# Down phase of a two-layer mixture of experts: expert 0 in the first pass, scaled one product ahead of its cast

## The chip, the cores and the metric

One core of one Trainium2 chip runs the kernel. The metric is the device time of one execution in microseconds; of several executions the median counts.

## The reference, cut to what matters

The kernel computes attention, a first mixture of experts in which each token goes to one expert, and a second one in which every token goes through all eight. The change touches only the second product of the second mixture:

```python
def _moe2_ref(x, w_gate, w1, w2):
    N, D = x.shape                      # 2304, 512
    E = w_gate.shape[1]                 # 8; F = 1024
    P = np.exp(x @ w_gate - ...)        # then 8 rounds of row and column scaling
    out = np.zeros((N, D), dtype=np.float32)
    for e in range(E):
        h = np.maximum(x @ w1[e], 0.0)
        ye = h @ w2[e]
        out += P[:, e:e + 1] * ye
    return out
```

## The kernel before, in words

The second mixture runs in two phases, each written as a two-by-two block product of Strassen's kind with seven products (numbered b = 0 to 6) in place of eight. The **up phase** makes h of all experts, and writes it to the DRAM tensor `hd`, which holds for each expert e, each third u of a token half and each b one block of 128 x 1536 floats (768 KB). For experts 1 to 7 the blocks are already scaled by the token's weight P and already combined to the operand that product b needs. For expert 0 the weights P are not known yet in the up phase: its four plain parts are stored (h11 under 0, h12 under 2, h22 under 6, h21 under 4), and the **down phase** scales and combines them.

The down phase runs from about 1327 us to the end. `PASS` splits the experts into two groups of four; within a pass the b's run in the order `DORD` = 0, 3, 1, 2, 4, 6, 5, within a b the four experts, and within an expert the thirds u = 0, 1, 2. `STEPS` lists (pass, b, expert), `SEQ` the 168 products (step m, third u), numbered n from 0; pass 1 is n = 0 to 83, pass 2 is 84 to 167, and each b has twelve products (b 0 of pass 1: 0 to 11, b 3: 12 to 23, b 1: 24 to 35, b 2: 36 to 47, b 4: 48 to 59, b 6: 60 to 71, b 5: 72 to 83; pass 2 the same from 84, except that the last two experts alternate in its last b). The products of the last of four experts in a b are so 9 to 11, 21 to 23, 33 to 35, 45 to 47, ... In the kernel before, expert 0 is the last of the second pass (in its last b, the first).

One product is 24 matmuls (line 1405): operands are split into a high part, made by a cast, and a residual, high x high first, then residual of the weight x high, then weight x residual of h. What feeds a product:

- `h_make(n)` (line 1280): takes the stage slot with product n's block, and calls `both` (line 939): ACT casts the high part into one of four buffers `D["h"]` (line 937), VectorE subtracts for the residual (line 941). For expert 0 it first combines and scales on VectorE (line 944, through `op2`): the "source work" below. `SRC` says which stored parts each b needs: one for b 0, 4, 6, two for b 3, 1, 2, 5. Scaled results that a later b needs are written back to `hd` on POOL's DMA queue (line 1298), and the next weights p are loaded on SyncE's queue (`p_load`, line 1101) into one of two buffers.
- `h_load(n)` (line 1268): issues loads from `hd` on SyncE's queue into the four stage slots in turn, up to four loads beyond product n's first. `h_make(n)` ends with `h_load(n + 1)`. A load waits until the slot's last readers are done: cast, residual, and a write-back from it.
- `w_make(m)` (line 1252): for b 3, 1, 2 and 6 a weight difference or sum on VectorE (line 944), then `both` for the weight block, into one of two buffers `D["w"]`.
- `merge` (line 1371): after the last expert of a b, VectorE adds the accumulated bank to the output blocks, at most two additions per product.

The order on each engine is the order in which the program calls these (no scheduler reorders them): in the loop's step n the matmuls of product n, then merges, then `h_make(n + 3)`, then, where u = 1, `w_make(m + 1)`, then weight loads.

The lines of the loop that set it:

```python
            h_make(n + 3)
            j = m % 4
            if m < NM - 3:
                if u == 1:
                    w_make(m + 1)
```

Of the kernel before, what the change touches and what calls it, by code (L numbers as in the profile page):

```python
# [13 lines left out]
ALU = mybir.AluOpType  # L14
# [4 lines left out]
B, H, S, D = 4, 8, 576, 64  # L19
# [78 lines left out]
def _program(ctx, tc, qT, kT, vv, tau, wg, mod, mbias, cst, wA, wg2, wU, wD, out):  # L98
# [3 lines left out]
    V, A, G = nc.vector, nc.scalar, nc.gpsimd  # L102
# [5 lines left out]
    hd = dram.tile([E, NU, 7, P, 4, UN], F32, name="hd")  # L108
# [50 lines left out]
    def bc(ap, shape):  # L159
        return ap.to_broadcast(shape)  # L160
# [614 lines left out]
    def experts(es):  # L775
# [157 lines left out]
        def copy_on(eng, out, in_):  # L933
            if eng is G:
                G.tensor_scalar(out=out, in0=in_, scalar1=1.0, scalar2=1.0, op0=ALU.mult, op1=ALU.mult)
            else:
                A.copy(out=out, in_=in_)  # L937

        def both(hi_lo, src, cp, sub):
            copy_on(cp, hi_lo[0], src)  # L940
            sub.tensor_tensor(out=hi_lo[1], in0=src, in1=hi_lo[0].bitcast(F32), op=ALU.subtract)  # L941

        def op2(eng, out, x, y, op):
            eng.tensor_tensor(out=out, in0=x, in1=y, op=op)  # L944
# [154 lines left out]
        def load_p(dst, e, u):  # L1099
            for t in range(2):  # L1100
                nc.sync.dma_start(
                    out=dst[t], in_=pd[t].rearrange("(e u t) n -> e u (t n)", e=E, u=NU)[e, u].partition_broadcast(P))
# [88 lines left out]
        def gates():  # L1191
# [18 lines left out]

        xs, steps, later = chained(xs, make_x(1), make_x(2)), gates(), sink()
        D = {}
        PASS = ((1, 2, 3, 4), (5, 6, 7, 0))
        DORD = (0, 3, 1, 2, 4, 6, 5)
        STEPS = [(i, b, e) for i, es4 in enumerate(PASS) for b in DORD
                 for e in (es4 if (i, b) != (1, 5) else es4[3:] + es4[:3])]
        NM = len(STEPS)
        SEQ = [(m, u) for m in range(NM - 2) for u in range(NU)] + [(m, u) for u in range(NU) for m in (NM - 2, NM - 1)]
        NB = len(SEQ)
        SRC = {0: (0,), 3: (6, 2), 1: (3, 0), 2: (2, 0), 4: (4,), 6: (6,), 5: (4, 1)}  # L1220
        LOADS = [(n, b) for n, (m, u) in enumerate(SEQ)
                 for b in (SRC[STEPS[m][1]] if STEPS[m][2] == 0 else STEPS[m][1:2])]
        FIRST = {}
        for i, (n, _) in enumerate(LOADS):
            FIRST.setdefault(n, i)
        SCALED = [n for n, (m, u) in enumerate(SEQ) if STEPS[m][2] == 0 and STEPS[m][1] in (0, 3, 2, 4, 6)]
        NST = 4
        loaded = [0]

# [18 lines left out]
        def w_load(i, j, k):  # L1248
            nc.sync.dma_start(out=D["blk"][j, k],
                              in_=wD[PASS[i][j], :, 1024 * k:1024 * k + 1024].rearrange("p (k n) -> p k n", k=4))  # L1250

        def w_make(m):
            if m >= NM:
                return
            i, b, e = STEPS[m]
            j = PASS[i].index(e)
            w11, w12, w21, w22 = (D["blk"][j, k] if (j, k) in D["blk"] else None for k in range(4))
            if b == 3:
                op2(V, w21, w11, w21, ALU.subtract)
            elif b == 1:  # L1260
                op2(V, w21, w22, w21, ALU.subtract)
            elif b == 2:
                op2(V, w11, w21, w11, ALU.add)
            elif b == 6:
                op2(V, w12, w12, w21, ALU.subtract)
            both(D["w"][m % 2], {0: w11, 3: w21, 1: w21, 2: w11, 4: w12, 6: w12, 5: w22}[b], A, V)

        def h_load(n):
            top = FIRST.get(n, len(LOADS)) + NST
            while loaded[0] < min(top, len(LOADS)):  # L1270
                k, b = LOADS[loaded[0]]
                m, u = SEQ[k]
                nc.sync.dma_start(out=D["stage"][loaded[0] % NST], in_=hd[STEPS[m][2], u, b])
                loaded[0] += 1

        def p_load(i):
            if i < len(SCALED):
                load_p(pbs[i % 2], 0, SEQ[SCALED[i]][1])

        def h_make(n):  # L1280
            if n < NB:
                m, u = SEQ[n]
                _, b, e = STEPS[m]
                x = D["stage"][FIRST[n] % NST]
                if e == 0:
                    y = D["stage"][(FIRST[n] + 1) % NST]
                    if b == 3:
                        op2(V, x, x, y, ALU.subtract)
                    if n in SCALED:
                        i = SCALED.index(n)  # L1290
                        op2(V, x, x, bc(pbs[i % 2][0 if b in (0, 4) else 1].unsqueeze(1), [P, 4, UN]), ALU.mult)
                        p_load(i + 2)
                    if b == 1:
                        op2(V, x, x, y, ALU.add)
                    elif b in (2, 5):
                        op2(V, x, x, y, ALU.subtract)
                    if b in (0, 3, 1, 4):
                        G.dma_start(out=hd[0, u, b], in_=x)  # L1298
                both(D["h"][n % 4], x, A, V)
                h_load(n + 1)  # L1300

        n_up = 2 * E * NU
        for n in range(n_up):
            k, u = divmod(n, NU)
            e, g = divmod(k, 2)
# [38 lines left out]
        def buf(tag=None):  # L1344
            if tag is None:
                tag = "ABCD"[turns[0] % 4]
                turns[0] += 1
            return (ps_d if tag == "D" else ps_m).tile([P, 2, 512], F32, tag=tag, name="r" + tag)
# [22 lines left out]
        def merge(i, b, u, q):  # L1371
            c11, c12, c21, c22 = quad[u]
            plus = lambda out, y=None: pend.append(lambda: op2(V, out, q, out if y is None else y, ALU.add))
            if b == 0:
                if i:
                    for c in quad[u]:
                        plus(c)
                else:
                    A.copy(out=c11, in_=q)
                    A.copy(out=c21, in_=q)  # L1380
            elif b == 3:
                plus(c22, None if i else c21)
                plus(c21)
            elif b == 1:
                plus(c12, None if i else c11)
                plus(c21)
                plus(c22)
            elif b == 2:
                plus(c12)
                plus(c22)  # L1390
            else:
                plus({4: c11, 6: c12, 5: c21}[b])
# [3 lines left out]
        for n, (m, u) in enumerate(SEQ):  # L1396
            i, b, e = STEPS[m]
            first, last = m % 4 == 0, m % 4 == 3
            if first:
                q[u] = buf()  # L1400
            a, h = D["w"][m % 2], D["h"][n % 4]
            for j, (l, r) in enumerate(((0, 0), (1, 0), (0, 1))):
                for i2 in range(2):
                    for k in range(4):
                        mm(q[u][:, i2, 0:UN], lhsT=a[l][:, k, 128 * i2:128 * i2 + 128], rhs=h[r][:, k],  # L1405
                           start=first and k == 0 and j == 0, stop=last and k == 3 and j == 2, skip_group_check=True)
            if last:
                merge(i, b, u, q[u][:, :, 0:UN])
            for _ in range(min(2, len(pend))):
                pend.pop(0)()  # L1410
# [5 lines that stand above are left out]
            elif m == NM - 3:  # L1416
                if u:
                    w_make(m + u)
            if (i, b) == (0, 0):
                w_load(0, j, (2, 3, 1)[u])  # L1420
            elif i == 0 and u == 2:
                if b == 4:
                    w_load(1, j, 0)
                elif b == 5:
                    w_load(1, j, 2)
                    w_load(1, j, 1)
                    if j == 0:
                        p_load(0)
                        p_load(1)
            elif (i, b) == (1, 0) and u == 2:  # L1430
                w_load(1, j, 3)
            if (i, b) == (1, 5):
                for _ in range(min(len(puts), 1 if n < NB - 4 else 2)):
                    put(*puts.pop(0))
                if last:
                    puts += [(u, 0, t) for t in range(3)]
# [15 lines left out]
    with tc.manual_schedule():  # L1452
        with ExitStack() as es:
            attention(es)
        with ExitStack() as es:
            experts(es)
# [88 lines left out]
```

## Time and profile before

| what | us |
|---|---|
| median of 3 runs (2090.96 to 2093.91) | 2091.51 |
| the profiled execution | 2093.61 |
| its span | 2091.8 |
| PE busy in it | 2007.3 (96%) |
| VectorE busy | 1559.2 (75%) |
| ACT busy | 873.0 (42%) |
| down phase, from PE's first product to the end | about 765 |

PE is TensorE's matmul stream, PEld its weight loads, DVE is VectorE, ACT ScalarE, POOL GpSimd, SP SyncE, which issues most DMAs. In a timeline a row is one instruction or several alike in a row: start, duration, engine, line, operation, tile written <- tiles read, shape, count; a bracket gives the time for which the engine stood idle before it and what ended that. `df` holds the stage slots (and some weight blocks), `dg`, `wr` and `x` weight blocks, `xa` and `w1c` the cast operands, `rA` to `rD` the accumulation banks, `pbx` the weights p.

### The profile page before, as it was taken

The numbers are of one execution on the slowest core, as the hardware profiler recorded it, in microseconds if no ns is written. First come the engines' busy times: TensorE is split into PE (matmuls) and PEld (weight loads), VectorE is DVE, ScalarE is ACT, GpSimd is POOL, SyncE is SP. The second block draws the span as 40 slices with busy tenths as digits, with TensorE's granted clock in tenths as the row PEclk, the third lists the DMA queues.
The fourth block names the chain that finished last, engine by engine and source line by source line (L and its number), as shares of the span: only waits on it lengthen the run. The fifth ranks groups of instructions, "written<-read, shape, count | busy, mean of one in ns | idle before, by whom it ended". The sixth has DMA issues, their size and how long they took to land.

```text
span 2091.8 us, 32577 instructions
## 1 busy us (share of the span) xinstructions
PE 2007.3 (96%) x12677; PEld 1911.2 (91%) x12677; DVE 1559.2 (75%) x1957; ACT 873.0 (42%) x1161; POOL 482.6 (23%) x395
## 2 busy tenths in 40 slices
PE   8999998999979999999999999999999999899997
PEld 6777778999969999999999999999999999899997
DVE  7788886666566789898989988856766568777672
ACT  6777763555554322222222222344444433433433
POOL 5564625051011233233333333000000000000003
PEclk9999998999999999999999999999999999999999
DMA  5232324666522576777676676965565676776753
GB/s 189 76 120 97 98 64 154 202 208 208 181 70 104 186 236 221 239 244 237 226 236 220 237 246 219 401 238 183 186 213 211 239 271 246 267 260 236 257 211 119
DMA packets 177214, 421.12 MB, mean 201 GB/s; under 512 B 16396, under 2 KB 126364, under 8 KB 177052
## 3 DMA queue, kind: packets, MB, share of 16 engines
q1 hardware_dynamic: 170700, 399.03, 55.9%
q0 software_dynamic: 4928, 19.93, 2.6%
q8 instruction: 102, 1.67, 0.3%
q14 instruction: 60, 0.49, 0.1%
q10 hardware_dynamic: 1424, 0.01, 0.0%
HBM read 274.91 MB, written 143.99 MB: 200 GB/s over the span
## 4 chain that ended last, share of the span: by engine, by line
PE 33%; issue 17%; DVE 13%; DMA 5%; ACT 2%; POOL 1%; SPq 0%; POOLq 0%; DVEq 0%; ACTq 0%
PE qA L1108 5%; PE qB L1108 5%; PE qC L1108 5%; DVE x L944 5%; PE rA L1405 5%; PE rB L1405 5%; PE rC L1405 4%; PE rD L1405 4%; DVE x L1112 4%; DMA pbx<-pd 2%; DVE w1c L941 2%; DVE xa L941 1%; DMA hd<-x 1%; POOL out L1363 1%; DVE df L944 1%
## 5 line engine op out<-in xcount | busy, mean ns | idle before, releaser
L944 POOL TENSOR_TENSOR x<-x 128x768 f32<-128x768 f32 x45 | 115.0, 2555 | 468.7 <-DVE x L1112 368.3
L941 DVE TENSOR_TENSOR xa<-df,xa 128x1536 fp32r<-128x1536 f32 (+1 forms) x100 | 166.6, 1670 | 62.0 <-ACT xa L937 61.5
L941 DVE TENSOR_TENSOR w1c<-df,w1c 128x1536 fp32r<-128x1536 f32 x84 | 146.3, 1756 | 88.2 <-ACT w1c L937 88.2
L937 ACT CAST xa<-df 128x1536 fp32r<-128x1536 f32 (+1 forms) x100 | 140.5, 1413 | 164.1 <-DVE df L944 69.5
L944 DVE TENSOR_TENSOR x<-x 128x768 f32<-128x768 f32 x135 | 196.3, 1454 | 4.9 <-DVE xb L944 0.5
L937 ACT CAST w1c<-df 128x1536 fp32r<-128x1536 f32 x84 | 123.7, 1481 | 143.5 <-DVE df L944 54.2
L1108 PE MATMUL qC<-xa,w1c 128*128 128x384 f32 x768 | 145.7, 338 | 3.8 <-ACT x L1156 3.6
L1108 PE MATMUL qA<-xb,w1c 128*128 128x384 f32 x768 | 146.1, 338 | 2.0 <-issue 1.8
L1298 POOL DMA_DIRECT2D hd<-df x12 | 6.6, 549 | 612.3 <-DVE df L944 612.3
L1108 PE MATMUL qB<-xc,w1c 128*128 128x384 f32 x768 | 143.6, 334 | 0.9 <-ACT x L1156 0.9
L478 DVE TENSOR_REDUCE cols<-s 128x1 f32<-128x576 f32 x144 | 105.0, 755 | 51.7 <-PE s L473 50.9
L1108 PEld LDWEIGHTS qA<-xb,w1c 128*128 128x128 f32 x768 | 136.2, 191 | 4.6 <-issue 3.4
L1108 PEld LDWEIGHTS qC<-xa,w1c 128*128 128x128 f32 x768 | 135.1, 190 | 4.4 <-ACT x L1156 4.0
L1108 PEld LDWEIGHTS qB<-xc,w1c 128*128 128x128 f32 x768 | 134.1, 188 | 1.3 <-ACT x L1156 1.3
L489 ACT ACTIVATE sa<-s,cols 128x576 f32<-128x576 f32 x144 | 103.5, 742 | 65.2 <-DVE cols L478 65.1
L1112 DVE SCALAR_TENSOR_TENSOR x<-x,pbx 128x768 f32<-128x768 f32 x126 | 125.8, 998 | 4.3
L473 PE MATMUL s<-colr 128*128 128x288 f32 x640 | 110.2, 310 | 4.7 <-DVE colr L432 1.3
L172 DVE TENSOR_TENSOR colr<-cols,colr 128x1024 fp32r<-128x1024 f32 x57 | 71.5, 1259 | 56.4 <-ACT colr L171 56.3
L1405 PE MATMUL rA<-xa 128*128 128x384 f32 x576 | 106.1, 339 | 5.7 <-ACT xa L937 5.7
L1405 PEld LDWEIGHTS rA<-xa 128*128 128x128 f32 x576 | 101.4, 190 | 6.6 <-ACT xa L937 6.6
L473 PEld LDWEIGHTS s<-colr 128*128 128x128 f32 x640 | 89.3, 190 | 19.2 <-issue 14.5
L1405 PE MATMUL rB<-w1c,xa 128*128 128x384 f32 x552 | 99.8, 335 | 0.0
(292 smaller groups left out, 4455.7 us busy)
## 6 DMA issues: line engine op xcount, KB each, us to landing
df<-hd SPq DMA_DIRECT2D x180, 768.0 KB, 4.5
hd<-x SPq DMA_DIRECT2D x317, 384.0 KB, 3.1
cols<-wA SPq DMA_DIRECT2D x84, 512.0 KB, 4.6
pbx<-pd SPq DMA_DIRECT2D x114, 192.0 KB, 5.1
wr<-wU SPq DMA_DIRECT2D x16, 768.0 KB, 6.3
dg<-wD SPq DMA_DIRECT2D x20, 512.0 KB, 7.1
hd<-df POOLq DMA_DIRECT2D x12, 768.0 KB, 8.0
cols<-qT SPq DMA_DIRECT2D x15, 576.0 KB, 3.9
```

The source lines that it names most:

```text
L172: sub.tensor_tensor(out=lo[i], in0=raw, in1=hi[i].bitcast(F32), op=ALU.subtract)
L473: mm(s[:, hf, 0:288], lhsT=l, rhs=r, start=n == 0, stop=n == len(ops) - 1)
L478: V.tensor_reduce(out=mx[:, i % 18:i % 18 + 1], in_=St[i][:, :, 0:288], axis=AX.XY, op=ALU.max, negate=True)
L489: A.activation(out=e.rearrange("p (h c) -> p h c", h=2), in_=St[i][:, :, 0:288], func=AF.Exp, bias=mxs[i // 18 % 2][0][:, i % 18:i % 18 + 1])
L937: A.copy(out=out, in_=in_)
L941: sub.tensor_tensor(out=hi_lo[1], in0=src, in1=hi_lo[0].bitcast(F32), op=ALU.subtract)
L944: eng.tensor_tensor(out=out, in0=x, in1=y, op=op)
L1108: mm(q[:, i, 0:UN], lhsT=a[l][:, k, 128 * i:128 * i + 128], rhs=b[r][:, k], start=first and k == 0 and j == 0, stop=k == nk - 1 and j == 2 ...
L1112: V.scalar_tensor_tensor(out=out, in0=src, scalar=0.0, in1=bc(pv.unsqueeze(1), [P, n, UN]), op0=ALU.max, op1=ALU.mult)
L1298: G.dma_start(out=hd[0, u, b], in_=x)
L1363: ins = G.indirect_dma_start(out=out, in_=o, in_offset=None, out_offset=bass.IndirectOffsetOnAxis(ap=idx_c[:, i:i + 1], axis=0))
L1405: mm(q[u][:, i2, 0:UN], lhsT=a[l][:, k, 128 * i2:128 * i2 + 128], rhs=h[r][:, k], start=first and k == 0 and j == 0, stop=last and k == 3 ...
```

## The change

Expert 0 moves from the end of the second pass to the end of the first: `PASS` becomes (1, 2, 3, 0), (4, 5, 6, 7), and the special order of experts in the last b goes. `h_make` is cut in two: `h_pre(n)` holds the source work of expert 0 (combining, scaling, write-back, next p load), and `h_make(n)` first calls `h_pre(n + 1)` and then casts product n, so that the source work is issued one product ahead of its cast. For b 2 the scaled h22 is now written back under 6, and the stored block 1 is subtracted from it into the other slot (`SRC[2]` is (6, 1) instead of (2, 0)); b 6 then loads that scaled block and isn't scaled again, which leaves 12 scalings instead of 15, and 15 write-backs instead of 12. The first two p loads move from the end of the first pass to behind product 2.

```diff
-        PASS = ((1, 2, 3, 4), (5, 6, 7, 0))
+        PASS = ((1, 2, 3, 0), (4, 5, 6, 7))
         DORD = (0, 3, 1, 2, 4, 6, 5)
         STEPS = [(i, b, e) for i, es4 in enumerate(PASS) for b in DORD
-                 for e in (es4 if (i, b) != (1, 5) else es4[3:] + es4[:3])]
+                 for e in es4]
-        SRC = {0: (0,), 3: (6, 2), 1: (3, 0), 2: (2, 0), 4: (4,), 6: (6,), 5: (4, 1)}
+        SRC = {0: (0,), 3: (6, 2), 1: (3, 0), 2: (6, 1), 4: (4,), 6: (6,), 5: (4, 1)}
-        SCALED = [n for n, (m, u) in enumerate(SEQ) if STEPS[m][2] == 0 and STEPS[m][1] in (0, 3, 2, 4, 6)]
+        SCALED = [n for n, (m, u) in enumerate(SEQ) if STEPS[m][2] == 0 and STEPS[m][1] in (0, 3, 2, 4)]
-        def h_make(n):
+        def h_pre(n):
             if n < NB:
                 m, u = SEQ[n]
                 _, b, e = STEPS[m]
...
                         p_load(i + 2)
                     if b == 1:
                         op2(V, x, x, y, ALU.add)
-                    elif b in (2, 5):
-                        op2(V, x, x, y, ALU.subtract)
-                    if b in (0, 3, 1, 4):
-                        G.dma_start(out=hd[0, u, b], in_=x)
-                both(D["h"][n % 4], x, A, V)
+                    if b in (0, 3, 1, 4, 2):
+                        G.dma_start(out=hd[0, u, 6 if b == 2 else b], in_=x)
+                    if b in (2, 5):
+                        op2(V, y, x, y, ALU.subtract)
+                        x = y
+                D[n] = x
+
+        def h_make(n):
+            if n < NB:
+                if n == 0:
+                    h_pre(0)
+                h_pre(n + 1)
+                both(D["h"][n % 4], D.pop(n), A, V)
                 h_load(n + 1)
...
+            if n == 2:
+                p_load(0)
+                p_load(1)
...
-                    if j == 0:
-                        p_load(0)
-                        p_load(1)
```

## Rows read from the trace of the kernel before

**Rows 1.** The page, engine summary: busy us, share of the span, instructions.

```profile
PE 2007.3 (96%) x12677; PEld 1911.2 (91%) x12677; DVE 1559.2 (75%) x1957; ACT 873.0 (42%) x1161; POOL 482.6 (23%) x395
```

**Rows 2.** Timeline of PE: start us, duration us, line, operation, count, [idle before <-releaser].

```profile
1423.67 4.32 PE L1405 MATMUL rD<-xa 128*128 128x384 f32 x24
...
1438.08 4.43 PE L1405 MATMUL rC<-xa 128*128 128x384 f32 x24 [1.75 <-ACT xa L937]
...
1475.63 4.32 PE L1405 MATMUL rC<-xa 128*128 128x384 f32 x24
...
1489.21 4.44 PE L1405 MATMUL rB<-xa 128*128 128x384 f32 x24 [0.93 <-ACT xa L937]
...
1527.10 4.32 PE L1405 MATMUL rB<-xa 128*128 128x384 f32 x24
...
1677.93 4.32 PE L1405 MATMUL rC<-xa 128*128 128x384 f32 x24
...
1784.31 6.04 PE L1405 MATMUL rA<-xa 128*128 128x384 f32 x24 [4.04 <-ACT xa L937]
...
1801.42 6.01 PE L1405 MATMUL rD<-xa 128*128 128x384 f32 x24 [2.75 <-ACT xa L937]
...
1856.69 5.84 PE L1405 MATMUL rC<-xa 128*128 128x384 f32 x24 [3.50 <-ACT xa L937]
...
1898.32 4.43 PE L1405 MATMUL rC<-xa 128*128 128x384 f32 x24 [2.51 <-ACT xa L937]
...
1914.36 4.63 PE L1405 MATMUL rB<-xa 128*128 128x384 f32 x16 [1.90 <-DVE xa L941]
...
2019.48 6.02 PE L1405 MATMUL rD<-xa 128*128 128x384 f32 x24 [3.74 <-ACT xa L937]
```

**Rows 3.** Windows: stretch, length, busy of PE, PEld, DVE, ACT, POOL; PEclk, DMA, GB/s.

```profile
1327.00:1384.00 57.00, 52.59 (x293) 51.95 (x291) 33.19 (x23) 21.03 (x18) 2.54 (x1) 0.97 0.88 340
...
1786.00:1788.00 2.00, 2.00 (x7) 2.00 (x7) 1.97 (x2) 0.00 (x0) 0.00 (x0) 0.50 0.49 195
```

**Rows 4.** Timeline of DVE and ACT around product 105, pass 2.

```profile
1768.27 1.75 DVE L944 TENSOR_TENSOR df<-df 128x1536 f32<-128x1536 f32 x1
...
1770.06 1.76 DVE L944 TENSOR_TENSOR df<-df,pbx 128x1536 f32<-128x1536 f32 x1
...
1773.44 1.76 DVE L941 TENSOR_TENSOR xa<-df,xa 128x1536 fp32r<-128x1536 f32 x1 [1.62 <-ACT xa L937]
...
1781.96 1.22 DVE L944 TENSOR_TENSOR dg<-df,dg 128x1024 f32<-128x1024 f32 x1
...
1783.21 1.04 ACT L937 CAST xa<-dg 128x1024 fp32r<-128x1024 f32 x1 [2.96 <-DVE dg L944]
```

**Rows 5.** Pass 2: waits of SP's queue (total, times, longest); timeline of SP, DVE.

```profile
SPq L1273 <- DMA hd<-df: 76.4, 12, 9.4
...
1833.78 0.80 SPq L1273 DMA_DIRECT2D df<-hd  x2
...
1842.13 1.76 DVE L944 TENSOR_TENSOR df<-df 128x1536 f32<-128x1536 f32 x1 [1.27 <-DMA df<-hd]
```

**Rows 6.** Timeline of DVE, pass 1: weight residuals two steps before each b's last expert.

```profile
1407.25 1.23 DVE L941 TENSOR_TENSOR xa<-dg,xa 128x1024 fp32r<-128x1024 f32 x1 [1.12 <-ACT xa L937]
...
1459.21 1.23 DVE L941 TENSOR_TENSOR xa<-dg,xa 128x1024 fp32r<-128x1024 f32 x1 [1.12 <-ACT xa L937]
...
1510.72 1.23 DVE L941 TENSOR_TENSOR xa<-df,xa 128x1024 fp32r<-128x1024 f32 x1 [1.12 <-ACT xa L937]
...
1659.13 1.22 DVE L941 TENSOR_TENSOR xa<-dg,xa 128x1024 fp32r<-128x1024 f32 x1
```

**Rows 7.** DMA issues from 1765, 1776, 1655: operation, count, KB, median us to landing.

```profile
df<-hd SPq DMA_DIRECT2D x1, 768.0 KB, 4.4
...
df<-hd SPq DMA_DIRECT2D x2, 768.0 KB, 5.6
...
df<-hd SPq DMA_DIRECT2D x6, 768.0 KB, 6.9
```

## Prediction, before the changed kernel was run

> **What bounds the kernel now.** I read the page's engine summary first: PE is busy 96% of the span [rows 1], so time can only be won or lost where PE stands still. The next view is PE's timeline of the down phase, one row per product. A product that follows another directly starts 4.16 us after it and shows 4.32 us; a bracket shows idle time ahead of it, and a longer duration is a slow restart [rows 2]. After the 4.04 us wait ahead of product 105 the granted clock is 0.50, the 1.2 GHz level, in the two microseconds shown [rows 3], and that product takes 6.04 us, 1.72 more. A stall therefore costs its idle time plus the excess over 4.32. Nearly every bracket names ACT's cast of a weight block. What that cast waits for is in VectorE's and ACT's timelines [rows 4]: for product 105 the weight difference (1781.96) stands in VectorE's queue behind the source work and residuals of products 105 and 106, and the cast (1783.21) follows it. So the bound at these places is VectorE's queue, in program order, with expert 0's extra work in it.
>
> **Gain: pass 2 loses expert 0.** Stalls that belong to it [rows 2]: 105 (4.04+1.72), 108 (2.75+1.69), 120 (3.50+1.52), 129 (2.51+0.11), 132 (1.90 plus 1.70, since its last 16 matmuls take 4.63 where 2.93 is usual) and 156 (3.74+1.70): 5.76+4.44+5.02+2.62+3.60+5.44 = 26.9 us. The places after b 3 and b 1 keep what pass 1 shows there without expert 0: 1.75+0.11 at product 24 and 0.93+0.12 at 36, 2.9 together. Gain: 24.0 us. Ends: 26.9 if these vanish too, 20 if a stall the size of 132's stays because another expert's merges take the place.
>
> **Scaling kept.** h22 is scaled once and stored, so three scalings of 1.76 us [rows 4] leave VectorE, 5.3 us, and with them six loads of weights p. All of that lies in b 6, where no stall is listed: nothing on the path. Three more stores go out on POOL's queue (15 for 12); POOL has no other work there, and they matter only through the stage slot that each holds (below). The stores make SyncE wait up to 9.4 us now [rows 5].
>
> **Expert 0 in pass 1, b 0, 4 and 6.** One source each, so loads are issued four products before use (16.6 us) and nothing waits for them. In b 0 the DMA engines are at 0.88 and 340 GB/s already [rows 3], and three stores and the moved p loads are added there; the cover is those 16.6 us less the longest typical load, 6.9 [rows 7]. I cost it at nothing; if the cover failed, about one load, 5 to 7 us. The first two p loads move on SyncE's queue from the end of pass 1 to behind product 2, three products (12.5 us) before VectorE asks for them: nothing. The removed swap of experts in the last b adds nothing beside the stall at 156 already counted.
>
> **The issue one product ahead: the large term.** There are four stage slots. For a product with two sources (b 3, 1, 2, 5) product n's pair and product n+1's pair fill all four. Loads go out on SyncE in order, each into the slot of the load four before it. So the second source of product n+1 can only be loaded after the residual of product n-1, and both sources of n+2 after the residual of n. Before, VectorE asked for them a whole product later: between residual n and the source work of n+2 lay source work and residual of n+1. Now it asks at once: VectorE's order becomes source work n0, residual n0-1, source work n0+1, residual n0, source work n0+2, residual n0+1, weight difference, weight residual (n0 is expert 0's first product). Source work n0+1 follows the very residual that frees its second load's slot, and n0+2 likewise. Both loads stand bare in VectorE's queue. Behind them stand the residual n0+1 and the weight work of the same step, and PE waits for that at product n0. The three-product lead of h does not help, because the weight's lead is shorter and its difference is queued behind the second wait.
>
> What the loads cost there is not shown directly. The nearest rows: a single load with stores around it landed in 4.4 us [rows 7]; in the stretch of b 5 loads land in 6.9 [rows 7]. For two at once, SyncE issued a pair at 1833.78 and VectorE, idle 1.27 us for it, could start at 1842.13, 8.35 us later, with a store going out at the same time [rows 5]; a pair of b 3 landed in 5.6 us in the median, 6.0 with the issue of the second [rows 7]. I take 5.0 for the single (near 4.4, with some store traffic) and 7.5 for the pair (nearer to 8.35, as a store is issued just before it here too).
>
> The sum for b 3, from the last weight residual before it, 1407.25+1.23 = 1408.5 [rows 6]: source work 3.55 (1768.27 to 1771.82 [rows 4]), 1412.05; residual 1.75, 1413.8; load 5.0, 1418.8; source work, 1422.35; residual, 1424.1; pair 7.5, 1431.6; source work, 1435.15; residual, 1436.9; weight difference 1.25, 1438.15; cast 1.1, 1439.25. Product 21 started at 1423.67 [rows 2]: 15.6 us late, and with a slow restart of 1.7 it is **17.3**. The store of the first product is out at 1412.3 and done after at most 9.4, 1421.7, before the residual at 1424.1: not the last wait.
> b 2 has the same lengths from 1510.72+1.23: cast done at 1542.7 against 1527.10, 15.6+1.7 = **17.3**.
> b 1 has one operation, 1.75, as source work: from 1460.45 the cast is done at 1485.8 against 1475.63, 10.2+1.7 = **11.9**.
> b 5 has one operation, no store and no weight difference, so its cast waits for nobody on VectorE; the weight residual ends at 1684.6 (from 1659.13+1.22 [rows 6]) and is wanted 8 matmuls, 1.39 us, into product 81, at 1679.3 [rows 2]: 5.3+1.7 = **7.0**.
> Together 53.5 us. After each such stall the merges again wait for PE's own ends, so the stalls at 24 and 36 stay as they are. The round trips between scaling, cast and residual that the edit removes (1.62 us each) are inside this replay: they are gone, and the loads are longer.
>
> Net: 53.5-24.0 = **+29.5 us**. The profiled execution took 2093.6 us (span 2091.8), 2.1 above the median of 2091.5; it becomes 2123.1, and the median 2121.
> Ends: with 4.4 and 6.0, 2.1 less at each of four places, 45.1; with 6.9 and 8.35, 2.75 more at each, 64.5. With the gain's ends that is +18 to +44.5: 2110 to 2136.
>
> The Trainium skill, "DMA: Bandwidth & Descriptors", section "Anatomy of one DMA", fits a transfer at about 2.0 us plus bytes over 436 GB/s (made for the software queue): for 768 KB an estimate of 3.8 us, for two 5.6, which would put the sum at about 2109. The trace disagrees, with 4.4 to 6.9 for the single load [rows 7], and decides.
>
> **Rivals.**
> *The loads are there in time* (not slower). If VectorE reached the next source work at least 5 us (single) and 7.5 us (pair) after the residual that frees the slot, only the gain would be left: 2091.5-24.0 = 2067. For it: before the change VectorE lost only 1.27 us to such loads in all of pass 2 [rows 5]. Against it: that cover was exactly one product's source work, cast and residual, which the edit takes away; no other instruction stands between. It decides at the slot's release: were a slot free earlier, this is the result. 8 in 100.
> *The order on the engines stays as it was* (the change doesn't do what it says). Then expert 0 costs in pass 1 what it cost in pass 2, and the time stays within a few us of 2091.5. Against it: each engine's order is the program's, and the diff moves the calls. 5 in 100.
> *Half of it*: VectorE waits, but one of the two loads is covered by merges or other weights' work standing in front. Without the single wait, 5.0 less at four places, +9.5: 2101. 9 in 100.
> *Worse than the sum*: the b 0 stretch runs out of DMA bandwidth (5 to 7 us), the restart after idle times near 15 us, which no row of the down phase shows, is longer than 1.7, or the store is still holding the slot: 5 to 15 us on top, 2126 to 2136 and beyond. 10 in 100, half of it beyond 2142.
>
> **How the numbers follow.** Forecast 68 in 100, 2121, between 2110 and 2138. To leave out no more than 2 in 10 the range must take in the half case and half of the worst: 2098 to 2142; outside are the first two rivals and 5 of the last, 18 in 100. A difference under about 0.2%, 4.2 us, can't be told from none. Faster by more than that: the first rival and a little of the second, 9 in 100; within it: 5; slower: 86.
>
> **What would show it.** Right: in pass 1 VectorE rows of line 944's kind idle for a load, twice at each of b 3, 1, 2 and 5, about 5 and 7.5 us; PE brackets of 10 to 16 us at products 21, 33 and 45 and some 5 at 81; none at 105, 129, 132 and 156; 15 stores, 12 scalings. Wrong: brackets of a few us at these four with VectorE busy, not idle, ahead of them (the order or the release of slots isn't as I read it), or stalls in pass 2 that don't go with expert 0.

## The result, and the profile after

| | before | after |
|---|---|---|
| median, us | 2091.62 | 2120.57 |
| profiled execution, us | 2093.61 | 2120.28 |
| its span, us | 2091.8 | 2118.5 |

The ratio after to before is 1.0138, 95% interval 1.0125 to 1.0152: the change makes the kernel 29 us slower. The forecast was 2121, so its sign and size came out; what had to be found out is whether its terms did.

PE's timeline of the kernel after, the products with idle time ahead of them (start, duration, line, operation, count, idle time and what ended it):

```profile
1332.16 4.46 PE L1413 MATMUL rB<-xa 128*128 128x384 f32 x24 [2.13 <-DVE x L1112]
1369.60 3.05 PE L1413 MATMUL rA<-xa 128*128 128x384 f32 x16 [2.47 <-DVE xa L941]
1383.77 4.46 PE L1413 MATMUL rD<-xa 128*128 128x384 f32 x24 [2.81 <-ACT xa L937]
1439.45 6.25 PE L1413 MATMUL rD<-xa 128*128 128x384 f32 x24 [17.93 <-ACT xa L937]
1455.78 6.01 PE L1413 MATMUL rC<-xa 128*128 128x384 f32 x24 [1.76 <-ACT xa L937]
1503.93 6.42 PE L1413 MATMUL rC<-xa 128*128 128x384 f32 x24 [8.85 <-ACT xa L937]
1519.61 4.43 PE L1413 MATMUL rB<-xa 128*128 128x384 f32 x24 [0.94 <-ACT xa L937]
1568.44 6.59 PE L1413 MATMUL rB<-xa 128*128 128x384 f32 x24 [10.79 <-ACT xa L937]
...
1727.51 5.49 PE L1413 MATMUL rC<-xa 128*128 128x384 f32 x16 [4.44 <-DVE xa L941]
...
1845.45 4.43 PE L1413 MATMUL rD<-xa 128*128 128x384 f32 x24 [1.63 <-ACT xa L937]
1896.52 4.43 PE L1413 MATMUL rC<-xa 128*128 128x384 f32 x24 [0.87 <-ACT xa L937]
```

The four long new stalls stand at products 21 (1439.45), 33 (1503.93), 45 (1568.44) and 81 (1727.51), where before PE ran through [rows 2]; a fifth, short one is at product 9 (1369.60). The brackets still name ACT's cast or VectorE's residual; what these waited for is in VectorE's timeline. Here is b 3, from the last weight residual before expert 0:

```profile
1404.93 1.22 DVE L941 TENSOR_TENSOR xa<-dg,xa 128x1024 fp32r<-128x1024 f32 x1 [1.11 <-ACT xa L937]
1406.07 1.75 DVE L944 TENSOR_TENSOR df<-df 128x1536 f32<-128x1536 f32 x1
1407.86 1.76 DVE L944 TENSOR_TENSOR df<-df,pbx 128x1536 f32<-128x1536 f32 x1
1409.53 1.75 DVE L941 TENSOR_TENSOR xa<-df,xa 128x1536 fp32r<-128x1536 f32 x1
1417.90 1.76 DVE L944 TENSOR_TENSOR df<-df 128x1536 f32<-128x1536 f32 x1 [6.62 <-DMA df<-hd]
1419.70 1.76 DVE L944 TENSOR_TENSOR df<-df,pbx 128x1536 f32<-128x1536 f32 x1
1421.37 1.75 DVE L941 TENSOR_TENSOR xa<-df,xa 128x1536 fp32r<-128x1536 f32 x1
1431.97 1.76 DVE L944 TENSOR_TENSOR df<-df 128x1536 f32<-128x1536 f32 x1 [8.84 <-DMA df<-hd]
1433.76 1.76 DVE L944 TENSOR_TENSOR df<-df,pbx 128x1536 f32<-128x1536 f32 x1
1435.43 1.75 DVE L941 TENSOR_TENSOR w1c<-df,w1c 128x1536 fp32r<-128x1536 f32 x1
1437.10 1.22 DVE L944 TENSOR_TENSOR dg<-df,dg 128x1024 f32<-128x1024 f32 x1
```

This is the predicted order, instruction by instruction: source work of product 21, residual of 20, **6.62 us for a load**, source work of 22, residual of 21, **8.84 us for a pair**, source work of 23, residual of 22, and only then the weight difference for which product 21 waits; ACT's cast follows at 1438.35 and PE at 1439.45. SyncE's timeline of the same stretch has the two issues, each right after the residual that frees the slot:

```profile
1411.31 0.32 SPq L1273 DMA_DIRECT2D df<-hd  x1
...
1423.15 1.42 SPq L1273 DMA_DIRECT2D df<-hd  x2
```

The sum over the phase is in VectorE's waits (total, times, longest), where the first line was 1.3 us, once, before:

```profile
DVE df L944 <- DMA df<-hd: 49.5, 12, 8.8
DVE df L944 <- DMA pbx<-pd: 7.9, 2, 5.5
```

### The profile page after: what moved, and what is told of

Its sections match the earlier page's. It is cut to its first block, busy times and chain, and to the rows that moved or that the text cites. A ratio compares the mean times of both kernels' runs of the same rounds, so it can differ in the third digit from the quotient of the medians.

```text
span 2118.5 us, 32588 instructions
## 1 busy us (share of the span) xinstructions
PE 2007.1 (95%) x12677; PEld 1910.4 (90%) x12677; DVE 1552.9 (73%) x1954; ACT 871.8 (41%) x1161; POOL 482.3 (23%) x398
## 4 chain that ended last, share of the span: by engine, by line
issue 28%; PE 22%; DVE 13%; DMA 6%; ACT 2%; POOL 1%; SPq 0%; DVEq 0%; POOLq 0%; ACTq 0%
PE qA L1108 5%; PE qB L1108 5%; PE qC L1108 5%; DVE x L944 5%; DVE x L1112 3%; DMA pbx<-pd 3%; DVE w1c L941 2%; DMA df<-hd 2%; PE rB L1413 2%; PE rC L1413 2%; PE rA L1413 2%; PE rD L1413 1%; DVE xa L941 1%; DMA hd<-x 1%; POOL out L1371 1%
## 5 line engine op out<-in xcount | busy, mean ns | idle before, releaser
L1371 POOL DMA_INDIRECT out<-df,kept x18 | 19.1, 1062 | 479.1 <-ACT df L1369 478.8
L1413 PE MATMUL rC<-xa 128*128 128x384 f32 x480 | 93.0, 351 | 15.9 <-ACT xa L937 11.5
L1413 PE MATMUL rB<-xa 128*128 128x384 f32 x504 | 93.4, 341 | 13.9 <-ACT xa L937 11.7
```

The costliest lines, as they stand in the source:

```text
L1371: ins = G.indirect_dma_start(out=out, in_=o, in_offset=None, out_offset=bass.IndirectOffsetOnAxis(ap=idx_c[:, i:i + 1], axis=0))
```

## The experiments

Times are medians; ratios are to runs of the kernel before on the same chip. A stall is counted as in the prediction: idle time plus what the product takes above 4.32 us (2.93 where 16 matmuls follow it).

**Undo the issue ahead alone.** Expert 0 stays in pass 1 and h22 stays kept.

```diff
-                if n == 0:
-                    h_pre(0)
-                h_pre(n + 1)
+                h_pre(n)
```

> The changed kernel with one part undone: expert 0's source work is issued in the same step as its cast again; expert 0 stays last in the first pass, the scaled h22 is still kept. Theory A (the issue one product ahead lays two loads bare in VectorE's queue): the four long PE waits at products 21, 33, 45 and 81 (19.9, 11.0, 13.1 and 7.0 us with their restarts) shrink to what expert 0 cost in pass 2 before, some 10, 4, 6 and a few us, so the time is near the kernel before, 2092 us (2085 to 2100). Rival B (the move into the first pass is what costs): it stays at 2115 to 2121.

2083.96 us, ratio 0.9964 [0.9953, 0.9976]: 36.6 us below the kernel after, a little below the kernel before, and a us below the range given. VectorE's waits and PE's timeline:

```profile
DVE df L944 <- DMA df<-hd: 4.8, 3, 2.5
```

```profile
1422.74 5.84 PE L1411 MATMUL rD<-xa 128*128 128x384 f32 x24 [2.79 <-ACT xa L937]
1440.10 7.26 PE L1411 MATMUL rC<-xa 128*128 128x384 f32 x24 [3.20 <-ACT xa L937]
1481.42 4.43 PE L1411 MATMUL rC<-xa 128*128 128x384 f32 x24 [0.77 <-ACT xa L937]
1499.31 6.75 PE L1411 MATMUL rB<-xa 128*128 128x384 f32 x24 [5.13 <-ACT xa L937]
1541.86 6.03 PE L1411 MATMUL rB<-xa 128*128 128x384 f32 x24 [2.51 <-ACT xa L937]
```

The load waits go from 49.5 to 4.8 us, and with them the long brackets. The five stalls shown, at 21, 24, 33, 36 and 45, come to 4.3+6.1+0.9+7.6+4.2 = 23.1 us, of which 2.9 (at 24 and 36) the kernel before has too [rows 2]: expert 0 costs some 20 us here, against 24 in pass 2. So neither pass is a bad place for it; rival B falls.

**Issue ahead alone, in the kernel before.** Expert 0 stays in pass 2, h22 is scaled twice.

```diff
-        def h_make(n):
+        def h_pre(n):
...
-                both(D["h"][n % 4], x, A, V)
-                h_load(n + 1)
+                D[n] = x
+        def h_make(n):
+            if n < NB:
+                if n == 0:
+                    h_pre(0)
+                h_pre(n + 1)
+                both(D["h"][n % 4], D.pop(n), A, V)
+                h_load(n + 1)
```

> The kernel before with one part of the change alone: source work one product ahead of its cast; expert 0 stays in pass 2 (first in its last b), 15 scalings, nothing kept. Theory A: the bare loads appear in pass 2, PE waits of 9 to 18 us at products 105, 117 and 129, and the time is 2118 us (2108 to 2126). Rival B (the move costs): 2092 us or less, some 2070 to 2092, because the round trips between scaling and cast are gone.

2123.2 us, ratio 1.0154 [1.0135, 1.0173]: all of the loss, with nothing moved. PE's timeline, at products 105, 117, 129 and in the last b, and VectorE's waits:

```profile
1800.14 6.35 PE L1412 MATMUL rA<-xa 128*128 128x384 f32 x24 [21.14 <-ACT xa L937]
...
1863.23 7.16 PE L1412 MATMUL rD<-xa 128*128 128x384 f32 x24 [9.07 <-ACT xa L937]
...
1927.29 5.95 PE L1412 MATMUL rC<-xa 128*128 128x384 f32 x24 [9.67 <-ACT xa L937]
...
2050.32 4.50 PE L1412 MATMUL rD<-xa 128*128 128x384 f32 x16 [6.47 <-DVE xa L941]
```

```profile
DVE df L944 <- DMA df<-hd: 42.6, 10, 8.7
```

The same stalls, in pass 2, at the same b's. With the run before it, this shows the issue ahead to be the cause: taking it out of the kernel after saves 36.6 us, putting it into the kernel before costs 32.

**Undo the kept h22 alone.** b 2 reads the stored blocks 2 and 0 again, b 6 scales again, 12 stores.

```diff
-        SRC = {..., 2: (6, 1), ...}
+        SRC = {..., 2: (2, 0), ...}
...
-        SCALED = [... STEPS[m][1] in (0, 3, 2, 4)]
+        SCALED = [... STEPS[m][1] in (0, 3, 2, 4, 6)]
...
-                    if b in (0, 3, 1, 4, 2):
-                        G.dma_start(out=hd[0, u, 6 if b == 2 else b], in_=x)
+                    if b in (0, 3, 1, 4):
+                        G.dma_start(out=hd[0, u, b], in_=x)
                     if b in (2, 5):
-                        op2(V, y, x, y, ALU.subtract)
-                        x = y
+                        op2(V, x, x, y, ALU.subtract)
```

> The changed kernel with the third part undone: h22 is scaled in b 3 as a source and again in b 6, b 2 reads the stored blocks 2 and 0, and there are 12 write-backs and 15 scalings again. Theory A (the kept h22 is off the path in b 6; in b 2 its three write-backs only lengthen the loads and hold the slots): b 6 shows no new stall from the three scalings of 1.76 us, and the stall at product 45 (10.8 us of idle time) shrinks by 1 to 4 us because no store is in flight: 2114 to 2121, near 2118. Rival B (the three scalings saved in b 6 were worth their 5.3 us): 2124 to 2128, with stalls at products 69 to 71.

2120.34 us, ratio 1.0146 [1.0127, 1.0164]: the same as the kernel after. PE's timeline, products 45 and 81, with one short bracket of b 6's beginning between them:

```profile
1568.54 5.77 PE L1412 MATMUL rB<-xa 128*128 128x384 f32 x24 [9.91 <-ACT xa L937]
1633.33 4.46 PE L1412 MATMUL rD<-xa 128*128 128x384 f32 x24 [0.77 <-ACT xa L937]
1726.00 5.49 PE L1412 MATMUL rC<-xa 128*128 128x384 f32 x16 [3.63 <-DVE xa L941]
```

The three scalings in b 6 make no stall, and without the three stores of b 2 the stall at 45 shrinks by only 1.7 us (13.1 to 11.4). The third part of the change is worth nothing that shows in the time. Theory A held, at the upper end of its range: I had given the stores in b 2 more weight than they have.

**Slots that are free earlier.** Two more stage slots for b 3, 1 and 5, in the places of one quarter of the weight blocks (one of each expert's four), which is therefore loaded later (during b 2, instead of in b 0 and around the end of pass 1); b 2 keeps four. A load is issued as soon as its slot's last user is done. Of the edit, the slots and the weight loads:

```diff
+            D["stage"] += [cut(dg, 8192, 4, UN), cut(wr, 0, 4, UN)]
...
-                w_load(0, j, (2, 3, 1)[u])
+                if u < 2:
+                    w_load(0, j, (2, 3)[u])
...
-                    w_load(1, j, 1)
...
+            if (b, u) == (2, 0):
+                w_load(i, j, 1)
```

> The changed kernel with two more stage slots for the products of b 3, b 1 and b 5 (in the places of one quarter of the weight blocks, which is then loaded during b 2), four as before for b 2. All order of instructions on VectorE stays. Theory A: no waits for loads at b 3, 1 and 5; from the replay without waits product 21 is still 3 us late (the weight work stands behind three products' source work), 33 and 81 not at all, and 45 keeps its 13 us; 2085 us (2078 to 2094). Rival C (VectorE's order and work, not the loads, make the long waits): 21, 33 and 81 stay within 3 us of 17.9, 8.9 and 4.4, and the time stays at 2115 to 2121.

2094.51 us, ratio 1.0015 [1.0004, 1.0026], half a us above the range given. PE's timeline: product 9, the next b's first, 21, and 45; nothing at 33 and 81:

```profile
1373.12 5.49 PE L1418 MATMUL rA<-xa 128*128 128x384 f32 x16 [3.39 <-DVE xa L941]
1390.06 7.25 PE L1418 MATMUL rD<-xa 128*128 128x384 f32 x24 [2.80 <-ACT xa L937]
1435.21 6.89 PE L1418 MATMUL rD<-xa 128*128 128x384 f32 x24 [4.63 <-ACT xa L937]
...
1552.04 6.54 PE L1418 MATMUL rB<-xa 128*128 128x384 f32 x24 [10.67 <-ACT xa L937]
```

Where the slots were added, the stalls go from 19.9, 11.0 and 7.0 to 7.2, 0 and 0; where they weren't (45) it stays: 12.9 against 13.1. The slot's release is what decides, as the rival "the loads are there in time" had it. The miss is at product 21 (7.2 us where 3 were expected), at product 9 (6.0 us against 2.6) and behind it (product 12: 5.73 against 2.95); VectorE's waits ahead of product 9 name the p loads: 10.9 us in two, one of 9.8.

**The later weight loads alone**, with four slots, as a control for the run above:

> The changed kernel, four slots, with one quarter of the weight blocks loaded during b 2 instead of b 0, which takes four of twelve 512 KB loads out of the stretch where the DMA engines move 398 GB/s. It is what the six-slot kernel has beside its slots. If that stretch's bandwidth makes the wait for the weights p and PE's 2.5 us at product 9, the time falls by 2 to 5 us, 2117 (2114 to 2119); if it is the place behind the other loads on the queue, it stays at 2119 to 2122. In both cases the waits at 21, 33, 45 and 81 stay: the six slots, not the late loads, took them away.

2113.86 us, ratio 1.012 [1.0095, 1.0144], just below the range given. They bring 4 to 7 us by themselves (by the ratios, whose intervals overlap, and by the medians). In its trace the bracket at product 9 is gone and those at 45 and 81 are smaller (8.80 and 2.10), while the stall at 33 is longer (12.7 us against 11.0). So the weight loads in b 0 cost about the 2.6 us at product 9; the rest lies at other places. Of the 26 us between the kernel after and the six slots some 20 are the slots.

**Weight work ahead of the h work of a step**, with the four slots of the kernel after:

```diff
-            h_make(n + 3)
             j = m % 4
             if m < NM - 3:
                 if u == 1:
                     w_make(m + 1)
...
+            h_make(n + 3)
```

> The changed kernel with the weight work of a step called ahead of the step's source work and cast, so that it no longer stands behind the second load; four slots, loads as bare as before. Theory A with its second half (the weight's place behind the wait is what PE feels): VectorE's waits for loads stay at about 50 us in total, but PE is late only for residuals, about 10 us at 21 or 22, 0 to 3 at 33 and 45, nothing at 81; and the small waits at the start of each b shrink by up to 1.75 us each. 2078 us (2070 to 2090). Rival (PE waits for h itself, not the weight): within 5 us of 2120.

2091.04 us, ratio 1.0003 [0.9993, 1.0013], at the upper end of what was expected and a us beyond. VectorE's waits, and PE's timeline in b 3:

```profile
DVE df L944 <- DMA df<-hd: 41.5, 11, 8.0
```

```profile
1422.64 6.69 PE L1413 MATMUL rD<-xa 128*128 128x384 f32 x24 [6.15 <-ACT xa L937]
...
1434.72 2.93 PE L1413 MATMUL rA<-w1c,xa 128*128 128x384 f32 x8 [2.60 <-DVE w1c L941]
...
1450.19 6.58 PE L1413 MATMUL rC<-xa 128*128 128x384 f32 x24 [8.23 <-ACT xa L937]
```

VectorE waits for its loads nearly as long as in the kernel after, but the pair's wait no longer stands ahead of the weight difference, and PE meets the waits one after the other: the single load's at product 21, the pair's at 22, and at 24 that of the next b's blocks, whose slots come free late (ACT's cast waits 8.17 us for one). The time is 29.5 us below the kernel after, but not all of that belongs to the load waits: the stalls at products 21 to 48, 81 and 82 fall from 55.7 to 38.2 us, 17.5 less, and the other 11 us are short stalls at product 9 and at the beginnings of b's, most of which the kernel before has as well. What the weight's place behind the load waits costs is therefore read from the next runs.

**Weight work first, in the other three settings**: in the kernel before; with the source work in its own step; and with the six slots.

> The kernel before with only the weight work called first. It says what that order is worth without the change. The waits at the first product of a b (0.8 to 2 us, eight places) go, and those of expert 0 at 105, 108, 120 and 129 shrink by what the weight stood behind: 2079 us (2072 to 2087). If the order is worth little without bare loads: 2088 to 2092.

2075.27 us, ratio 0.9931 [0.9909, 0.9954], within the range given: the order alone is worth 14.7 us without the change.

> Expert 0 in the first pass, h22 kept, source work in the step of its cast (as in the first run), and the weight work called first. Theory A: this has no bare loads and no weight behind them; of the first run's waits at 21 to 48 (some 20 us with restarts) half goes, and the small ones in pass 2: 2071 us (2064 to 2079), below both kernels. If the two orders undo each other, as in the weights-first run: 2082 or more.

2071.31 us, ratio 0.9907 [0.9891, 0.9924], as expected. With the weight work first, the issue ahead thus costs 2091.04-2071.31 = 19.7 us, where in the order of the kernel before it costs 36.6. A little under half of its cost hangs on the weight's place behind the load waits; the rest stays with the waits themselves.

> Both edits together: two more stage slots for b 3, 1 and 5, and the weight work of a step called first. Theory A: neither the loads nor the weight's place holds PE at 21, 33 and 81; 45 (four slots) keeps 2 to 7 us; the wait of some 8 us at 24 that the weights-first kernel showed goes, since it came from loads held up behind full slots; the small waits at the start of each b stay away. 2073 us (2066 to 2082), below the kernel before. Rival (the reordering only shifts the same wait): 2088 or more.

2061.29 us, ratio 0.9858 [0.9841, 0.9875]: some 5 us below the range given, and the best version found. VectorE still waits in it, 6.2 us for blocks (three waits) and 11.6 for p (two), but the longest stall of PE behind product 1 is 7.0 us, at 45, where there are four slots.

**Six slots and weight work first, without the issue ahead**, to see whether the idea of the change is worth anything once its loads are covered:

> The six-slot version with the weight work first (2061.3), with the source work put back into the step of its cast. It tells whether issuing ahead is worth anything once its loads are covered. Theory A (the issue ahead costs only through its loads, and with a slot free early it saves VectorE's turn between scaling, cast and residual ahead of the first product): 2066 to 2073, near 2069, since the same-step version with four slots, at 2071.3, loses almost nothing to loads (2.5 us of VectorE's time) and so gains little from two slots more. Rival B (the six slots and the later weight loads alone make the 2061, and the issue ahead is worth nothing): 2059 to 2064.

2070.02 us, ratio 0.9904 [0.9888, 0.992]: as expected, and 8.7 us above the version that issues ahead, with intervals that don't meet. So the issue ahead is worth something once its loads are covered; with four slots that is lost under 50 us of waits. That it is the round trip in VectorE's queue which is saved is argued, not shown. The two traces place about 6 of the 8.7 us: from product 2 on the stalls come to 16.0 against 10.3 (7.1 at 24, 3.9 at 47 and 4.1 at 48, against 7.0 at 45 and 2.0 at 48, and 1 us or less at 39 and 99). The rest of the 10.2 us by which the two spans differ lies ahead of product 2, and whether it comes from the kernels or from the two executions stays open.

## Why the prediction was right

**What bounds the kernel** held: every new stall leads from PE, over ACT's cast or directly (9 and 81), to VectorE's queue.

**The gain in pass 2** held: 24.0 predicted. The six stalls of [rows 2] are gone, and of the two places that were to keep theirs, 108 keeps 1.63+0.11 and 120 keeps 0.87+0.11 (predicted 1.86 and 1.05): 26.9-2.7 = 24.2.

**The loss** held in its mechanism at all four places, and as a sum within 2.6 us; by place it was 2.6 too small, 1.0 and 4.2 too large, and right:

| product | predicted | measured |
|---|---|---|
| 21 (b 3) | 17.3 | 17.93+1.93 = 19.86 |
| 33 (b 1) | 11.9 | 8.85+2.10 = 10.95 |
| 45 (b 2) | 17.3 | 10.79+2.27 = 13.06 |
| 81 (b 5) | 7.0 | 4.44+2.56 = 7.00 |
| sum | 53.5 | 50.9 |

- *The loads of b 3 were sized too small.* The single one cost 6.62 us of idle time and the pair 8.84, where I took 5.0 and 7.5. I gave b 1 and b 5 the same two lengths, and there they were a little too long: 4.85 and 6.90 in b 1, 4.33 and 5.79 in b 5 (VectorE at 1713.67 and 1722.89). VectorE's timeline of b 1:

```profile
1487.91 1.76 DVE L944 TENSOR_TENSOR df<-df 128x1536 f32<-128x1536 f32 x1 [4.85 <-DMA df<-hd]
1498.23 1.76 DVE L944 TENSOR_TENSOR df<-df 128x1536 f32<-128x1536 f32 x1 [6.90 <-DMA df<-hd]
```

  The stores of b 1 go out at the same points as those of b 3, but nothing is scaled there and no p is loaded. In b 3 SyncE issues p loads right around the blocks' loads (at 1409.64 and 1411.67 beside the single, at 1421.48 and 1424.67 beside the pair), and I put them nowhere. The pair's wait is 1.8 to 2.1 us longer in b 3 than in b 1 in all four versions that issue ahead with four slots and the h work first (8.67 to 8.84 against 6.63 to 6.90). This speaks for the p loads; no run takes them out alone. The Trainium skill, "DMA: Bandwidth & Descriptors", section "Anatomy of one DMA", gives by its fit for the software queue an estimate of 3.8 us for 768 KB and 5.6 for two; the waits in b 5, 1 and 3, of 4.33 to 6.62 and 5.79 to 8.84 us, are all longer.
- *b 2 was sized too large.* I gave it b 3's lengths. But its first operation there is the scaling, which needs one source only, so it runs while the second is still on its way. VectorE's timeline of b 2 after the change, and SyncE's issue of the pair:

```profile
1549.05 1.75 DVE L944 TENSOR_TENSOR df<-df,pbx 128x1536 f32<-128x1536 f32 x1
1553.47 1.76 DVE L944 TENSOR_TENSOR df<-df 128x1536 f32<-128x1536 f32 x1 [2.67 <-DMA df<-hd]
...
1560.26 1.76 DVE L944 TENSOR_TENSOR df<-df,pbx 128x1536 f32<-128x1536 f32 x1 [3.36 <-DMA df<-hd]
1562.75 1.76 DVE L944 TENSOR_TENSOR df<-df 128x1536 f32<-128x1536 f32 x1 [0.73 <-DMA df<-hd]
...
1551.24 6.00 SPq L1273 DMA_DIRECT2D df<-hd  x2
```

  The single load costs 2.67 and the pair 3.36+0.73 = 4.09, with one more wait of 1.68 ahead of them. The pair is no longer issued together either: the diff writes b 2's operand into the other slot, so the first slot is free before the residual, and SyncE's row spans an issue at 1551.24 and one at 1556.92, where the residual ends. The first load landed 8.9 us after its issue, so this gained little; with h22 scaled twice both go out behind the residual (1556.41), and the pair costs 4.41+0.30, nearly the same. The diff shows the order of the operations; the step that failed is "b 2 has the same lengths".
- *The restart* was 1.9 to 2.6 us, not 1.7, after these longer gaps: part of the rival "worse than the sum", at under 1 us a stall.

**"I cost b 0 at nothing"** was wrong by 2.6 us: product 9 waits 2.47. The windows view of its stretch (columns as in [rows 3]) and VectorE's timeline:

```profile
1325.00:1383.00 58.00, 51.37 (x294) 50.41 (x292) 38.17 (x26) 20.78 (x18) 4.35 (x4) 1.00 1.02 398
```

```profile
1350.92 1.76 DVE L944 TENSOR_TENSOR df<-df,pbx 128x1536 f32<-128x1536 f32 x1 [2.47 <-DMA pbx<-pd]
...
1364.98 1.76 DVE L944 TENSOR_TENSOR df<-df,pbx 128x1536 f32<-128x1536 f32 x1 [5.47 <-DMA pbx<-pd]
```

The DMA engines went from 0.88 and 340 GB/s [rows 3] to 1.02 and 398. The cover of 16.6 us held for the expert's blocks but for one wait of 1.73; what came late were the small p loads, which share this full stretch with the weight loads. I gave the first two a lead of 12.5 us; SyncE issued them from 1341.31 on and VectorE asked at 1348.45, 7.1 us later. The third, at which I had not looked, needs the buffer that product 9's scaling frees (1352.7): issued at 1352.71, it landed 12.2 us later, and the weight residual for which product 9 waits stands behind the scaling that needs it. It is the large term's mechanism once more, with the two p buffers in place of the slots. The run with later weight loads agrees: no bracket there, and the longest wait for p is 3.8 us. So does the run without the issue ahead, in which VectorE waits 5.9 us for p and PE has no bracket at product 9.

**The kept h22 at nothing** held, by its own run.

**The net.** 50.9+2.6-24.2 = 29.3 us in the rows named. The spans differ by 26.7: the phase's first products come 1.9 us earlier in the profiled run of after, product 1 restarts 1.6 us faster there (4.46 against 6.02), and the restarts at products 12 and 24 trade 1.6 us each way. In the versions whose order of weight work is that of the kernel before, product 1 started anywhere between 1331.5 and 1334.4 us and took 4.4 to 6.0, though they are alike up to there; so I read these as differences between executions. The medians differ by 29.0, the prediction said 29.5. The mechanism and the size of the loss were forecast; that the median came out within half a us of 2121 is luck, since errors of 1 to 4 us of either sign cancelled, and the profiled execution, which the sum put at 2123.1, took 2120.3.

The rival "the loads are there in time" is what the six slots make of it at 33 and 81; with the weight work first as well the time came to 2061 us, under the 2067 that the rival gave.

## What to carry to other kernels

Before an instruction is issued earlier on an in-order engine, look at what frees the buffer that its input is loaded into: if that is an instruction that it now follows directly, the load's whole time stands bare in the queue, and a deep prefetch elsewhere doesn't help. Then ask what is queued behind it, since the price is paid by the operand with the shortest lead, here the weight block; putting that operand's work first was worth 13 to 33 us in all four settings tried. The issue ahead paid only with it and with two slots more; with the slots alone it was not compared. Cost each load site by which of its sources the first instruction really reads, and by what other loads stand around it.

## What was not expected of the hardware

In these traces a restart is not longer the longer PE stood still: it cost 1.93 us after 17.93 in the kernel after, 1.69 after 1.76 (product 24, with nothing like it at that place before: 0.11 after 1.75 [rows 2]), and 2.94 after 3.20 in the version with the source work in its own step. In that last case the granted clock was 0.50 from 1440.1 to 1446 us, nearly 6 us; in the kernel after, behind 17.93 us, it was 0.50 from 1439.45 to 1443.4 and 0.99 in the next 2 us. With the DMA engines at 398 GB/s, a wait for a p load of 192 KB reached 5.5 us; in the six-slot version (388 GB/s) it was 9.8, where VectorE's longest wait for a 768 KB block in the whole phase was 4.3.
